# The fifth row block of x^T phi(k) in branch A: seven 64-column products ahead of KV instead of one 128-column pass

## The chip, the cores and the metric

One core of one Trainium2 chip runs the kernel. The metric is the device time of one execution in microseconds; the time before is the median of three runs. The engines are named as in the profile: PE is the matrix engine (PEld its weight loads), DVE the vector engine, ACT the scalar engine, POOL the general one, SP the engine that here only issues transfers. L12 is line 12 of the kernel before.

## The reference

Two linear-attention blocks over the same input x (2048 rows, 640 features, 32 heads of 20) are mixed by a gate:

```python
qkv = (x @ wqkv).reshape(B, S, 3, H, Dh).transpose(2, 0, 3, 1, 4)
q, k, v = qkv
phi = lambda t: where(t > 0, t + 1, exp(t)) + 1e-6
pq, pk = phi(q), phi(k)
kv = einsum("bhsd,bhse->bhde", pk, v)
z = pk.sum(over s)
num = einsum("bhqd,bhde->bhqe", pq, kv)
den = einsum("bhqd,bhd->bhq", pq, z) + 1e-6
block = (num / den).reshape(B, S, D) @ wo
...
g = sigmoid((x * gate_w).sum(-1))
out = g * block_A + (1 - g) * block_B
```

## The kernel before

The sum over the rows, phi(k)^T v, is not taken from v: since v = x wv, the kernel forms G = x^T phi(k), 640 by 640, and then KV = (wv block)^T G for each head group. A head needs only its own 20 columns, so KV is small: six column groups k, each of 60 + 60 or 40 + 40 columns, in 60 products with stationary operands of 60 or 40 columns (`kv_mm`, L457). The two halves of a group lie in the left and the right half of the array's columns (`tile_position=(0, 0)` and `(0, 64)`).

The stages of branch A, in the order of PE's queue:

- k chunks (`k_chunk`, L227): for each of 16 row chunks, 10 products of 320 columns into a PSUM slot, and phi of it. ACT takes the exponential; then either DVE reads the slot again (an unlifted chunk: one `tensor_scalar` and one `scalar_tensor_tensor`), or ACT writes t + 1 (a lifted one, L209) and DVE takes the maximum in SBUF.
- q units (`q_unit`, L275): 10 products of 512 columns each, phi in the same way. The last five units of A stand ahead of G.
- G. The rows of G are the features of x: five blocks of 128. The first four are made by a Strassen-Winograd scheme (`g_strassen`, L375): two by two blocks of x (row half by 256 features) and of phi(k) (row half by 320 columns), seven products of 16 matmuls instead of eight, with sums of x blocks (`x_sum`, S3 and part of MB) and of phi(k) blocks (`k_sum`, in the free buffer pqTB) made on DVE. The fifth block is made the plain way by `g_pass` (L307): 16 row chunks by 2 column halves, 32 matmuls of 320 columns (tile gA). Between its chunks stand `z_pass` (the sums z, tile zA) and DVE's work on them; `rec_pass` (L516) forms the denominators (denA, 40 products four abreast), DVE adds the gate and takes the reciprocal in two halves (`rec(0)`, `rec(1)`), and these go through DRAM into R, which is spread over the partitions.
- `scale` (L576) multiplies phi(q) by R on DVE, in the stage of G and among B's first chunks.
- B's k chunks follow. After the second stands `kv_a` (L480), A's KV with its mask on DVE, and from the fifth on every other chunk is followed by a pair of products for M = KV wo (`m_a`).

Branch B goes through the same stages, and the output is made from both by seven products for each pair of row blocks (`Pair`).

PSUM is one pool of four slots of two banks each (`ps`, L66); a tile in a slot waits until the readers of the one before it are done. k chunks, q units and M products take the slots in turn; the G stage names them. The code in `tc.manual_schedule()` runs in the order in which it is written; each engine goes through its own queue in order. Ahead of everything PE runs seven warm-up products on constants (L164).

Of the kernel before, what the change touches and what calls it, by code (L numbers as in the profile page):

```python
# [8 lines left out]
P = 128  # L9
# [7 lines left out]
DT = D // P  # L17
# [3 lines left out]
HB = 512  # L21
# [11 lines left out]
def kernel(  # L33
# [21 lines left out]
    psum = banks.enter_context(tc.tile_pool(name="psum", bufs=1, space=bass.MemoryType.PSUM))  # L55

    turn = [0]

    def ps_raw(name, slot=None):

        if slot is None:
            slot = turn[0]
            turn[0] = (slot + 1) % 4
        return psum.tile([P, 4 * HB], BF16, tag=f"ps{slot}", name=name)
# [9 lines left out]
    GT2 = persist.tile([P, 2 * DT, HF], BF16, name="GT")  # L74
    GT = [GT2[:, n * DT:(n + 1) * DT, :] for n in range(2)]
# [19 lines left out]
    SX[4] = flat(M[1], "p c d -> p (c d)", ic)  # L95
    TK = [{k: flat(pqT[1], "p c s -> p (c s)", HF, k - 1) for k in (1, 2, 3, 4)}, {}]
# [67 lines left out]
    for n in (HB,) * 6 + (HB // 2,):  # L164
        nc.tensor.matmul(warm[:, 1, 0:n], lhsT=one_l, rhs=one_r[:, 0:n], start=True, stop=True)
# [141 lines left out]
    def g_pass(b, c, slot):  # L307

        pt = ps(f"g{'AB'[b]}", slot)
        for i in range(ST):  # L310
            if b == 0 and i == 4:
                gate_exp()
            if i == (8 if b else 13):
                zsel = z_pass(b)
                if b:
                    p_diff(part[0])
                else:
                    x_sum(2)
                    gate_done(0)
            if b == 1 and i == 13:  # L320
                p_diff(part[1])
# [12 lines left out]
    def x_sum(k, cuts=(0, hc)):  # L334

        x11, x21 = [xn[:, 0:hc, n:n + ic] for n in (0, ic)]
        x12, x22 = [xn[:, hc:ST, n:n + ic] for n in (0, ic)]
        a, b, op = {
            1: (x21, x22, ALU.subtract), 2: (x11, SX[1], ALU.subtract),
            3: (x21, x11, ALU.subtract), 4: (x12, SX[2], ALU.subtract),  # L340
        }[k]
        for lo, hi in zip(cuts, cuts[1:]):
            add_rows(SX[k][:, lo:hi], a[:, lo:hi], b[:, lo:hi], op)
# [21 lines left out]

    def g_prod(pt, left, right, first, lo=0, hi=hc):
# [8 lines left out]
    def g_strassen(b, den):  # L375

        x11, x12 = [xn[:, k:k + hc, 0:ic] for k in (0, hc)]
        x22 = xn[:, hc:ST, ic:2 * ic]
# [4 lines left out]
        def temp(name):  # L383
            return work.tile([P, 2, HF], FP32, tag="osb", name=name, bufs=3)
# [5 lines left out]
        g_prod(even, x11, b11, True, 0, 1 - b)  # L390
        rec = den()
        rec(0)
        g_prod(even, x11, b11, True, 1 - b)
        p1 = temp("p1")
        nc.scalar.copy(out=p1[:], in_=even[:, :, 0:HF])
        if b == 0:
            x_sum(3)
        else:
            rec(1)
        g_prod(odd, SX[2], TK[b][2], True)  # L400
        u2 = temp("u2")
        add(u2[:], odd, p1)
        if b == 0:
            x_sum(4)
        else:
            p_diff(part[2])
            p_diff(part[3])
            m_sum(0)
        g_prod(even, x12, b21, False)
        nc.scalar.copy(out=lo[:, 0:2, :], in_=even[:, :, 0:HF])  # L410
        if b == 0:
            rec(1)
        r_load(b, 1, nc.scalar)
        if b == 0:
            wq[1] = load_w(1, "q", nc.scalar)
        scale(b, 0, 2, 0)
        g_prod(odd, SX[3], TK[b][3], False)
        u3 = temp("u3")
        add(u3[:], odd, p1)
        scale(b, 2, 4, 0)  # L420
        even = ps("gs0", 0)
        g_prod(even, SX[1], TK[b][1], True)
        if b == 1:
            load_wo(1, nc.sync)
        add(hi[:, 2:4, :], even, u3)
        scale(*((b, 0, 2, 1) if b else (b, 4, 5, 0)))
        g_prod(odd, x22, TK[b][4], False)
        if b == 1:
            scale(1, 4, 5, 0)
        add(lo[:, 2:4, :], odd, p1)  # L430
        if b == 1:
            scale(1, 2, 4, 1)
# [3 lines left out]
        if b == 0:  # L436
            scale(0, 0, 2, 1)
    def z_pass(b):
# [454 lines left out]
```

## Time and profile before

| | us |
|---|---|
| runs | 182.18, 182.56, 182.52 (median 182.52) |
| the profiled execution's own time | 182.66 |
| its span | 180.9 |
| k chunks of A from the ninth, and q units, to | 49.2 |
| G of A, 49.2 to | 70.2 |
| B's k chunks with A's KV and M, to | 94.7 |
| B's q units, to | 116.3 |
| G of B, to | 137.3 |
| output, last product to | 177.5 |

All times in the profile are counted from the start of its span. A row of the timeline gives the start, the length, the engine, the line, the operation and its operands; several of one kind in a row are one row with a count. A product's row is longer than the time it holds the array up: products of 320 columns last 299 ns each in the record and follow one another every 136 ns.

### The profile page before, as it was taken

The page shows a single profiled execution, that of the slowest core. Times are in us where ns is not written, and L with a number is a line of the kernel's source. Part 1 is how long each engine was busy: PE and PEld are TensorE (multiplying, and loading weights), DVE is VectorE, ACT ScalarE, POOL GpSimd, SP SyncE. Part 2 cuts the span into 40 slices and gives each one's busy share as a digit, 9 for nine tenths or more (in the row PEclk, how much of TensorE's full clock was granted, in tenths as well). Part 3 has the DMA queues.
Part 4 walks back from the last instruction along what each step waited for, and adds up shares of the span by engine and source line. Part 5 has one row for each costly group of instructions (what it writes and reads, how often), then busy time and mean ns, then how long its engine had stood idle before and what let it go on. Part 6 is the DMA issues. An engine that isn't in the chain of part 4 may idle for free.

```text
span 180.9 us, 3415 instructions
## 1 busy us (share of the span) xinstructions
PE 176.8 (98%) x1340; PEld 119.3 (66%) x1345; DVE 147.6 (82%) x247; ACT 85.8 (47%) x140; POOL 5.4 (3%) x18
## 2 busy tenths in 40 slices
PE   8999999999999999999999999999999999999993
PEld 4565657765577777777775555577777777777772
DVE  0386868989999896888778999969999799977863
ACT  2245846889972101378784779931101763111010
POOL 6000000000000000000000000000002300000000
PEclk9999999999999999999999999999999999999999
DMA  5999999524100217331115000000325451133323
GB/s 183 214 261 170 240 364 297 110 38 145 58 0 5 72 32 226 91 127 35 57 34 186 23 0 0 0 0 18 112 79 144 129 179 60 36 109 112 109 92 127
DMA packets 22842, 19.33 MB, mean 107 GB/s; under 512 B 10538, under 2 KB 22058, under 8 KB 22826
## 3 DMA queue, kind: packets, MB, share of 16 engines
q1 hardware_dynamic: 20744, 16.95, 34.0%
q10 hardware_dynamic: 2082, 2.17, 3.7%
q8 instruction: 10, 0.16, 0.4%
q14 instruction: 6, 0.05, 0.1%
HBM read 12.29 MB, written 4.53 MB: 93 GB/s over the span
## 4 chain that ended last, share of the span: by engine, by line
PE 95%; DMA 2%; issue 0%; DVE 0%; ACTq 0%
PE gs L370 17%; PE kA L218 12%; PE ox L590 12%; PE kB L218 12%; PE qB L281 12%; PE qA L281 6%; PE oz L590 6%; PE qA L291 5%; PE gA L329 2%; PE gB L329 2%; DMA wkA<-in_A_wqkv_dram 2%; PE ow L590 2%; PE qA L301 1%; PE mA L494 1%; PE s L494 1%; PE oy L590 1%
## 5 line engine op out<-in xcount | busy, mean ns | idle before, releaser
L218 PEld LDWEIGHTS <-xT 128*128 128x128 bf16 x320 | 31.0, 98 | 13.1 <-DVE xT L243 0.8
L210 DVE TENSOR_SCALAR e<-e 128x640 bf16<-128x640 bf16 (+2 forms) x53 | 18.9, 357 | 7.2 <-ACT e L205 6.6
L218 PE MATMUL kA<-wkA,xT 128*128 128x320 bf16 (+1 forms) x160 | 22.8, 300 | 0.3 <-DMA wkA<-in_A_wqkv_dram 0.3
L218 PE MATMUL kB<-wkB,xT 128*128 128x320 bf16 x160 | 23.1, 299 | 0.0
L281 PE MATMUL qB<-xT,wqB 128*128 128x512 bf16 x98 | 21.6, 379 | 0.1
L205 ACT ACTIVATE e<-kB 128x640 bf16<-128x640 f32 x16 | 11.3, 704 | 15.8 <-DMA wqB<-in_B_wqkv_dram 9.4
L281 PEld LDWEIGHTS <-wqB 128*128 128x128 bf16 x100 | 11.7, 117 | 9.7
L205 ACT ACTIVATE e<-kA 128x640 bf16<-128x640 f32 x16 | 11.2, 705 | 8.4 <-PE kA L218 8.4
L205 ACT ACTIVATE e<-qA 128x1024 bf16<-128x1024 f32 (+1 forms) x11 | 10.4, 946 | 6.4 <-PE qA L291 5.1
L648 ACT COPY u<-ox 128x320 f32<-128x320 f32 x8 | 3.4, 426 | 20.4 <-PE ox L590 20.4
L205 ACT ACTIVATE e<-qB 128x1024 bf16<-128x1024 f32 x10 | 10.2, 1024 | 5.6 <-PE qB L281 4.9
L370 PEld LDWEIGHTS <-xn 128*128 128x128 bf16 x96 | 9.2, 98 | 3.9 <-issue 0.4
L370 PEld LDWEIGHTS <-S 128*128 128x128 bf16 x96 | 9.4, 98 | 3.6
L281 PE MATMUL qA<-xT,wqA 128*128 128x512 bf16 x49 | 10.9, 379 | 0.1
L214 DVE SCALAR_TENSOR_TENSOR pk<-kB,e 128x640 bf16<-128x640 f32 x12 | 9.9, 825 | 1.3
L590 PEld LDWEIGHTS <-xT 128*128 128x128 bf16 x85 | 8.1, 98 | 2.9
L590 PEld LDWEIGHTS <-pqTB 128*128 128x128 bf16 x80 | 7.8, 98 | 3.2
L590 PEld LDWEIGHTS <-pqTA 128*128 128x128 bf16 x80 | 7.7, 98 | 2.9
L370 PE MATMUL gs<-pk,xn 128*128 128x320 bf16 x64 | 9.5, 299 | 0.0
L281 PEld LDWEIGHTS <-wqA 128*128 128x128 bf16 x50 | 5.9, 117 | 4.8
L291 PE MATMUL qA<-xT,wqA 128*128 128x512 bf16 x38 | 8.9, 379 | 0.1
L212 DVE TENSOR_TENSOR pk<-pk,e 128x640 bf16<-128x640 bf16 x12 | 5.9, 492 | 2.8 <-ACT pk L209 2.2
(123 smaller groups left out, 297.1 us busy)
## 6 DMA issues: line engine op xcount, KB each, us to landing
xn<-in_A_x_dram SPq DMA_DIRECT2D x1, 2240.0 KB, 9.7
out_dram<-pk SPq DMA_DIRECT2D x14, 160.0 KB, 1.8
wvA<-in_A_wqkv_dram SPq DMA_DIRECT2D x1, 800.0 KB
wkB<-in_B_wqkv_dram SPq DMA_DIRECT2D x1, 800.0 KB, 4.6
wqB<-in_B_wqkv_dram ACTq DMA_DIRECT2D x1, 800.0 KB, 5.0
wvB<-in_B_wqkv_dram SPq DMA_DIRECT2D x1, 800.0 KB
MA<-mA_dram SPq DMA_DIRECT2D x1, 800.0 KB, 5.5
MB<-mB_dram SPq DMA_DIRECT2D x1, 800.0 KB
```

Of the source, the lines that this page charges most:

```text
L205: nc.scalar.activation(out=e[:], in_=src, func=ACT.Exp)
L210: nc.vector.tensor_scalar(e[:], e[:], 1.0, EPS, op0=ALU.min, op1=ALU.add)
L212: nc.vector.tensor_tensor(out=dst, in0=dst, in1=e[:], op=ALU.max)
L214: nc.vector.scalar_tensor_tensor(out=dst, in0=src, scalar=1.0 + EPS, in1=e[:], op0=ALU.add, op1=ALU.max)
L218: nc.tensor.matmul(pt[:, hf, 0:w], lhsT=xT[:, c, i * P:(i + 1) * P], rhs=wk[b][:, c, hf * HF:hf * HF + w], start=(c == 0), stop=(c == DT - 1),
L281: nc.tensor.matmul(pt[:, u, :], lhsT=mixed(wq[b][:, c, :], m), rhs=xT[:, c, n * HB:(n + 1) * HB], start=(c == 0), stop=(c == DT - 1),)
L291: nc.tensor.matmul(pt[:, u, :], lhsT=mixed(wq[b][:, c, :], m + u), rhs=xT[:, c, n * HB:(n + 1) * HB], start=(c == 0), stop=(c == DT - 1),)
L329: nc.tensor.matmul(pt[:, hf, 0:HF], lhsT=xn[:, i, c * P:(c + 1) * P], rhs=pk[:, i, hf * HF:(hf + 1) * HF], start=(i == 0), stop=(i == ST - 1),
L370: nc.tensor.matmul(pt[:, n, 0:HF], lhsT=left[:, i, n * P:(n + 1) * P], rhs=right[:, i, :], start=(first and i == 0), stop=(i == hc - 1), s ...
L494: nc.tensor.matmul(dst[:w, 0:HF], lhsT=KVA[:rows, k, 0:w], rhs=wo_sb[b][:rows, k, n * HF:(n + 1) * HF], start=True, stop=True,)
L590: nc.tensor.matmul(dst, lhsT=left[:, c, r0:r0 + P], rhs=right[:, c, :], start=(first and c == 0), stop=(c == DT - 1), skip_group_check=not ...
L648: nc.scalar.copy(out=self.u6[:], in_=self.at("x"))
```

## The change

The diff's core; the rest are shifts of names that follow from it.

```diff
-    psum = banks.enter_context(tc.tile_pool(name="psum", bufs=1, space=bass.MemoryType.PSUM))
+    def psum_pool(stack, name, slots, **how):
+        pool = stack.enter_context(tc.tile_pool(name=name, bufs=1, space=bass.MemoryType.PSUM, **how))
+        pools.update({slot: pool for slot in slots})
+    psum_pool(banks, "low", (2, 3))
+    high = ExitStack()
+    psum_pool(high, "high", (0, 1))
...
-    GT2 = persist.tile([P, 2 * DT, HF], BF16, name="GT")
+    GT2 = persist.tile([P, 2 * (DT + 1), HF], BF16, name="GT")
+    SN = {k: flat(M[0], "p c d -> p (c d)", P // 2, k - 1) for k in (1, 2, 3, 4)}
...
-    for n in (HB,) * 6 + (HB // 2,):
+    for n in (HB // 2,) * 13:
...
+    def narrow_sums():
+        for k in (1, 2, 3, 4):
+            x_sum(k, f0=2 * ic, w=P // 2, dst=SN)
...
+    def g_a(single):
+        odd, even = two("o"), two("e")
+        third = ps("gs2", 2)
+        p1 = g_temp("p1")
+        gate_exp()
+        for n in prod(even, x11, b11, True):
+            nc.scalar.copy(out=p1[:, n], in_=even[n])
+        g_prod(third, SX[1], t[1], True, 0, 5)
+        zsel = z_pass(0, 3)
+        x_sum(2)
+        gate_done(0)
+        g_prod(third, SX[1], t[1], True, 5)
+        rec = rec_pass(0, zsel, 3)
+        rec(0)
+        x_sum(3)
+        for n in prod(even, x12, b21, False):
+            nc.scalar.copy(out=lo[:, n, :], in_=even[n])
+        wq[1] = load_w(1, "q", nc.scalar)
+        u2 = g_temp("u2")
+        for n in prod(odd, SX[2], t[2], True):
+            add(u2[:, n], odd[n], p1[:, n])
+        x_sum(4, 0, hc // 2)
+        u3 = g_temp("u3")
+        for n in prod(odd, SX[3], t[3], False):
+            add(u3[:, n], odd[n], p1[:, n])
+            if n == 0:
+                x_sum(4, hc // 2, hc)
+        for n in range(2):
+            add(hi[:, 2 + n], third[:, n, 0:HF], u3[:, n])
+        for n in prod(odd, x22, t[4], False):
+            add(lo[:, 2 + n], odd[n], p1[:, n])
+        rec(1)
+        g_prod(third, SX[4], b22, False)
+        for n in range(2):
+            add(hi[:, n], third[:, n, 0:HF], u2[:, n])
+        r_load(0, 1, nc.sync)
+        x11, x12, _, x22 = x_blocks(2 * ic, P // 2)
+        def narrow(pt, left, right, first):
+            for i in range(hc // 2):
+                for r in range(2):
+                    rows = slice(r * P // 2, (r + 1) * P // 2)
+                    j = r * hc // 2 + i
+                    nc.tensor.matmul(
+                        pt[rows, :], lhsT=left[:, j, :], rhs=right[:, j, :], start=(first and i == 0),
+                        stop=(i == hc // 2 - 1), tile_position=(0, rows.start), skip_group_check=not first,
+                    )
+        A, B = two("e")
...
+        narrow(A, x11, b11, True)
+        nc.scalar.copy(out=p1, in_=A)
+        narrow(B, SN[2], t[2], True)
+        nc.scalar.copy(out=u6, in_=B)
+        C, G = two("o")
+        narrow(C, x12, b21, True)
+        add(lo[:, DT - 1, :], C, p1)
+        narrow(A, SN[1], t[1], False)
+        nc.scalar.copy(out=p15, in_=A)
+        narrow(B, SN[3], t[3], False)
+        add(hi[:, DT, :], B, p15)
+        narrow(G, SN[4], b22, True)
+        add(v, u6, p15)
+        add(hi[:, DT - 1, :], G, v)
+        kv = ps("kvA", 2)[:, 0]
+        wide = range(DT - 1)
+        kv_step(kv, (0,), wide, True)
+        narrow(B, x22, t[4], False)
+        add(lo[:, DT, :], B, p1)
+        kv_step(kv, (1, 2, 3, 4, 5), wide)
+        kv_step(kv, (0, 1, 2), (DT - 1,))
+        kv_step(kv, (3, 4, 5), (DT - 1, DT))
+        kv_step(kv, (0, 1, 2), (DT,))
+        kv_mask(kv)
...
+    def load_narrow():
+        src = A_wqkv[2 * ic:D, 2 * D:3 * D].rearrange("(n p) f -> p n f", n=2)
+        for r in range(2):
+            nc.sync.dma_start(out=wv[0][r * P // 2:(r + 1) * P // 2, DT - 1:DT + 1, :], in_=src)
...
+        if n:
+            k_sum(0, 1)
...
-                k_sum(0, 1)
+                narrow_sums()
...
-        g_all(0)
-        turn[0] = 3
+        high.close()
+        with late_pool("halves") as halves:
+            g_a(lambda name, n: bank(halves, f"{name}{n}"))
+        psum_pool(banks, "again", (0, 1), reuse_waits="tile")
+        turn[0] = 0
+        scales = {1: (0, 0), 2: (1, 0), 3: (2, 0), 4: (3, 0), 5: (4, 0), 7: (0, 1), 9: (1, 1), 10: (2, 1), 11: (3, 1), 13: (4, 1)}
         for i in range(ST):
-            k_chunk(1, i, lifted=i in (5, 7, 9, 13))
-            if i in (3, 5, 7):
-                scale(0, i // 2 + 1, i // 2 + 2, 1)
+            k_chunk(1, i, lifted=i in (1, 2, 3, 5, 7, 9, 11, 13))
+            if i in scales:
+                c, h = scales[i]
+                scale(0, c, c + 1, h)
             if i > 3 and i % 2 == 0:
                 m_a(i // 2 - 2)
             if i == 1:
-                kv_a()
                 wv[1] = load_w(1, "v", nc.sync)
```

In words. The fifth block (features 512 to 639) is cut into two halves of 64 features and goes through the same seven-product scheme as the other four. A narrow product adds over the eight row chunks of a row half, but four of them go into the left half of the array's columns and four into the right (`r`), so each PSUM tile holds two partial sums on 64 partitions each; eight matmuls of 320 columns make a product, 56 the whole block, against 32 before. The partial sums are added by KV itself: `load_narrow` puts the 64 rows of wv on both halves of the partitions, and the fifth block fills two row tiles of GT, so KV has 72 products instead of 60. The four differences of narrow x blocks lie in the buffer of MA (SN); they are made where the first sum of phi(k) blocks was, which moves ahead of A's second q blocks.

KV no longer stands between B's chunks but directly behind the narrow products, with its first eight matmuls ahead of the seventh of them. The wide products write one-bank tiles (`halves`, laid over slots 0 and 1, in which the first tiles used are those of slot 1; the last q unit is in slot 0), and each half of a product is read by itself. The order around zA is another: the 26 products ahead of zA are now the first wide product and part of a second, and six products instead of eight lie between zA and denA. All rescaling of phi(q) goes behind B's chunks, ten pieces of one row tile and one half each; four more of these chunks are lifted. The second half of R is stored and loaded through SP's queue instead of ACT's, and B's wq is issued earlier on ACT. In the output, the stores of pairs 1 and 2 take both their row blocks in one transfer, and the temporaries u6 and v share one tile. Branch B's G is unchanged.

More of the change, by code (lines that the diff above doesn't have):

```diff
@@ L310, in g_pass @@
         for i in range(ST):
[L311 to L320, printed above, removed]
+            if i == 8:
+                zsel = z_pass(b, 0)
+                p_diff(part[0])
+            if i == 13:
                 p_diff(part[1])
@@ L364, in z_last, with g_half @@
         add_rows(Z[:, 0, 0:HF], Z[:, 0, 0:HF], Z[:, 0, HF:D], ALU.add)
+    def g_half(pt, left, right, n, first, lo=0, hi=hc):
+        for i in range(lo, hi):
+            nc.tensor.matmul(
+                pt, lhsT=left[:, i, n * P:(n + 1) * P], rhs=right[:, i, :],
+                start=(first and i == 0), stop=(i == hc - 1), skip_group_check=not first,
+            )
     def g_prod(pt, left, right, first, lo=0, hi=hc):
@@ new lines, in kv_step @@
+    def kv_step(dst, ks, cs, fresh=False):
+        for k in ks:
+            for c in cs:
+                for p0, hf, d0, w in kv_groups(k):
+                    nc.tensor.matmul(
+                        dst[p0:p0 + w, k * WT[0]:k * WT[0] + w], lhsT=wv[0][:, c, hf * HF + d0:hf * HF + d0 + w],
+                        rhs=GT[hf][:, c, d0:d0 + w], start=(fresh and k == ks[0] and c == cs[0]), stop=(c == cs[-1]),
+                        tile_position=(0, p0), skip_group_check=True,
+                    )
```

140 lines of the change are left out of this document (75 added, 65 removed).

## The prediction

> **What bounds the kernel now.** I read the page from the top: the busy shares, then the chain that ended last, then TensorE's waits, and only then the stage that the change rewrites.
>
> ```profile
> PE 176.8 (98%) x1340; PEld 119.3 (66%) x1345; DVE 147.6 (82%) x247; ACT 85.8 (47%) x140; POOL 5.4 (3%) x18
> ...
> DVE  0386868989999896888778999969999799977863
> ...
> PEclk9999999999999999999999999999999999999999
> ...
> PE 95%; DMA 2%; issue 0%; DVE 0%; ACTq 0%
> ...
> PE xt L165 <- PEq L877: 0.8, 1, 0.8
> PE kA L218 <- DMA wkA<-in_A_wqkv_dram: 0.3, 1, 0.3
> ```
>
> TensorE (PE) is busy for 98% of the span, its clock is granted in full in every slice, and 95% of the chain is its own work. The last two lines are all that its view of waits holds: 1.1 us, both before 6 us. From there to the last product PE never waits. So the time can only fall by work taken from PE, and it can rise by any new wait on PE's queue, however small. VectorE (DVE), at 82%, is the engine that could make one.
>
> The stretch that is rewritten, from the chain in order of time (start, length, what):
>
> ```profile
> 1.24 4.19 DMA wkA<-in_A_wqkv_dram
> ...
> 49.17 3.53 PE gA L329 x26
> 52.70 0.17 PE zA L442 x5
> 52.88 0.82 PE gA L329 x6
> 53.70 0.27 PE gs L370 x2
> 53.98 1.21 PE denA L177 x40
> 55.18 15.05 PE gs L370 x110
> 70.23 2.72 PE kB L218 x20
> 72.94 0.96 PE kvA L462 x60
> 73.91 4.18 PE kB L218 x30
> ```
>
> The fifth row block is gA: 32 full products, 3.53 + 0.82 = 4.35 us, 136 ns each. KV is 60 small products, 0.96 us.
>
> **Part 1: the seven narrow products.** They replace 32 products of 320 columns by 56 whose stationary operand has 64 columns, two of them side by side in the array's column halves. If a pair runs at once, that is 28 pair times for 32. No row shows a 64-column pair of 320; these are the nearest:
>
> ```profile
> 53.91 0.95 PE L177 MATMUL denA<-pqTA,zsel 128*32 128x256 bf16 x28
> ...
> 53.91 1.28 PE L177 MATMUL denA<-pqTA,zsel 128*32 128x256 bf16 x40
> ...
> 72.37 0.57 PE L218 MATMUL kB<-wkB,xT 128*128 128x320 bf16 x3
> ...
> 72.88 0.51 PE L462 MATMUL kvA<-GT,wvA 128*60 128x60 bf16 x22
> ...
> 72.88 1.03 PE L462 MATMUL kvA<-GT,wvA 128*60 128x60 bf16 x60
> ```
>
> The first two rows are the same run of products cut at two places: 12 more take 0.33 us, and they go four abreast, so a round of 256 columns takes 110 ns. One product alone costs 136 ns for 320 columns, 0.43 ns a column; 64 columns more make a round of 320 columns 0.110 + 0.028 = 0.138 us. I take 0.137 us a pair. The other end is the pair one after the other, 0.272 us; denA, which shares the array in the same way, stands against that. 28 x 0.137 = 3.84 us: a saving of 0.51 us, the only one in the change.
>
> **Part 2: KV grows from 60 to 72 products**, because the block now has six row tiles. By the last two rows 38 of them take 0.52 us, 13.7 ns each; 12 more cost 0.17 us (0.19 by 0.96/60). The kB row (0.57 us, three products) puts its third start at 72.64 and kvA's first at 72.88: 0.24 where 0.136 is usual, so entering the split array costs 0.1 us. That is paid once before, at KV, and once after, at the first narrow product, since KV follows in the same form. It is no term.
>
> **Part 3: denA comes two products sooner.** Before, eight products lie between zA and denA (0.82 + 0.27 us); after, six, because the two gs products moved ahead of zA.
>
> ```profile
> 52.27 0.42 DVE L210 TENSOR_SCALAR e<-e 128x1024 bf16<-128x1024 bf16 x1
> ...
> 52.79 0.69 DVE L212 TENSOR_TENSOR pqTA<-pqTA,e 128x1024 bf16<-128x1024 bf16 x1
> ...
> 53.40 0.32 DVE L446 TENSOR_TENSOR zsel<-zA,headE 128x160 bf16<-128x160 f32 x1
> ...
> 53.90 0.99 PEld L177 LDWEIGHTS <-zsel 128*32 128x32 bf16 x40 [0.26 <-DVE zsel L446]
> ```
>
> zsel stands behind the last q unit's work on DVE and cannot come sooner. It ends at 53.72, and its readers began at 53.90. PE would be ready 0.27 us earlier than before, at 53.63. So denA waits between 0.09 us (started at 53.72) and 0.27 (at 53.90); I take 0.18. Behind it in PE's queue stands the whole rest of the stage. The first products themselves wait for nothing: their banks lie where the second q unit was read long ago.
>
> **Part 4: the narrow results must be read while PE runs on.** Five DVE adds and three ACT copies now stand between the products and KV, and two products write banks that must be read first.
>
> ```profile
> 61.80 1.75 DVE L530 RECIPROCAL rT<-d 128x256 bf16<-128x256 f32 x1
> ...
> 70.27 0.89 DVE L435 TENSOR_TENSOR GT<-gs,u 128x320 bf16<-128x320 f32 x2 [1.35 <-PE gs L370]
> ...
> 167.75 0.84 PE L590 MATMUL ox<-TM,xT 128*128 128x320 bf16 x5
> ...
> 167.91 0.48 DVE L595 TENSOR_TENSOR pk<-ox,xn 128x320 bf16<-128x320 f32 x1
> ...
> 168.63 0.43 ACT L648 COPY u<-ox 128x320 f32<-128x320 f32 x1 [2.29 <-PE ox L590]
> ...
> 169.08 0.49 DVE L595 TENSOR_TENSOR v<-u,xn 128x320 f32<-128x320 f32 x1 [0.29 <-ACT u L648]
> ```
>
> A result is read 0.2 us after PE could go on (168.63 less the fifth start, 167.75 + 0.54, less 0.136), an add takes 0.48, a copy 0.43. Count from the first narrow product, 0.55 us each. The second reciprocal goes ahead of this on DVE: it starts at about -1.5, when the wide product before last has been added (-2.18 + 0.2 + 0.48), and with 0.42 us of preparation ends at +0.67; two adds of the wide block end at 1.56. The third product's result is due at 1.84, so 0.28 us are spare. The fifth product ends at 2.74, its add runs 2.94 to 3.42. PE has done the sixth product and eight KV products by 3.40 and starts the seventh at 3.48, with 0.06 for the signal: 0.08 late. DVE then does v, the sixth and the seventh's add, to 4.87; PE reaches the last six KV products at 4.83 and needs 4.93. Together 0.17 us; 0 if DVE overlaps its instructions, as the pair at 70.27 does (0.89 for two), and each 0.1 us that DVE is later beyond the spare costs 0.1.
>
> **Part 5: the rescaling of phi(q) leaves this stage** and goes, in ten pieces, behind B's k chunks. There DVE must keep within four PSUM slots of PE.
>
> ```profile
> 79.76 0.70 ACT L205 ACTIVATE e<-kB 128x640 bf16<-128x640 f32 x1 [0.35 <-PE kB L218]
> ...
> 81.18 0.49 DVE L212 TENSOR_TENSOR pk<-pk,e 128x640 bf16<-128x640 bf16 x1 [0.36 <-ACT pk L209]
> ...
> 81.59 0.69 DVE L579 TENSOR_TENSOR pqTA<-pqTA,R 128x1024 bf16<-128x1024 bf16 x1
> ...
> 82.20 0.32 DVE L210 TENSOR_SCALAR e<-e 128x640 bf16<-128x640 bf16 x1
> ...
> 82.62 0.82 DVE L214 SCALAR_TENSOR_TENSOR pk<-kB,e 128x640 bf16<-128x640 f32 x1
> ...
> 95.89 0.82 DVE L214 SCALAR_TENSOR_TENSOR pk<-kB,e 128x640 bf16<-128x640 f32 x1
> ```
>
> Start to start, a piece takes 0.61, a lifted chunk 0.83 and another 1.22 us, against PE's 1.36 a chunk and 0.27 for each M product. A lifted chunk that is not held up is done 2.03 us after PE (79.76 less 0.2, to 81.59). From chunk 1 on this lag grows: chunk 4 is at 2.66, chunk 5 at 2.47, chunk 6, not lifted and behind two pieces, at 2.94 and 0.08 for signals. Its slot is wanted 2.99 us after it was filled, by the third M product: 0.03 us late; I take 0.05. Later lags stay under 2.9, and the last chunk is lift-bound or level as before (95.89 + 0.82), so B's q pass starts from the same state. ACT has 0.35 us idle in every chunk pair for the four added lifts.
>
> **Part 6: what costs nothing.** The thirteen warm-ups stream the same 3,328 columns as the seven.
>
> ```profile
> 0.84 2.93 PE L165 MATMUL xt<-const-bfloat16-1.0 128*128 128x512 bf16 x7 [0.84 <-PEq L877]
> ...
> 3.42 1.15 PEld L239 LDWEIGHTS <-xn 128*128 128x128 bf16 x10 [0.35 <-DMA xn<-in_A_x_dram]
> ```
>
> Behind them PE waits for x, and the chain there is the load of wkA, to 5.43. Were they 0.3 us longer, that load would still cover them. The Trainium skill ("TensorE: Matmul & The Clock Gate", Part 1) says that the clock opens after some 3.4 us of activity, whatever the number of matmuls; by it too this part is zero. The narrow copy of wv (two more transfers of 160 KB, with wvA cut to 640) follows wo on SP's queue, ahead of B's wk, and is wanted only at the last KV products. R's second store and load go from ACT's queue to SP's, ahead of wvB, which only B's KV reads; R itself is wanted at B's chunk 7, some ten us after its reciprocal. The narrow differences (four of 512 elements) take the place of the first k sum on DVE, which moves into the sixth slice, where DVE is busy six tenths; were there no room, it would pass through four PSUM slots before PE felt it. In the output, u6 and v share a tile with three buffers where each had two, and the stores of pairs 1 and 2 go out together, on a queue for which PE never waits.
>
> **The sum:** -0.51 + 0.17 + 0.18 + 0.17 + 0.05 = +0.06 us. The profiled execution took 182.66 us for a span of 180.9, so 182.72; against the median of the three runs, 182.52, it is 182.6. Less PE work, given back as waits.
>
> **The rivals.**
> *Faster:* the waits of parts 3 to 5 all fall away and a pair costs 0.133: -0.62 + 0.17 = -0.45, 182.1 us. For it speaks that DVE's back-to-back instructions overlap; against it that zsel is bound by DVE. Chance 0.17.
> *Slower, by the weight loads:* each pair needs two 64-column loads; if they can't run ahead in the split array they are added. zA's five products with full weights and 32 columns take 0.17 us, 34 ns each, so unhidden loads cost at most about 34 ns a pair: 28 x 0.171 = 4.79, and the sum is +1.0, 183.5 us. It decides above 0.148 us a pair. denA, whose loads were hidden, is against it. Chance 0.10. The Trainium skill speaks for this one: "TensorE: Matmul & The Clock Gate", Part 3, under what overlaps and what doesn't, lets a weight load run under a product only where the two use other rows of the array, and a column pair uses all of them. The trace does not agree for denA, whose rounds of 110 ns leave no room for four loads.
> *Slower, by DVE's queue at the reciprocal:* if the split adds leave DVE 0.9 us later than part 4 has it, the spare 0.28 is gone and KV ends 0.6 late: 183.2 us. It decides from 0.6 us of delay. Chance 0.15.
> *The pairs don't run together:* 56 x 0.136 = 7.6, +3.8, 186.4 us. Chance 0.03.
> *The backlog in B's chunks* passes on 0.1 us or more at each M product: 183.1 us. Chance 0.05.
>
> **How the numbers follow.** My own case has 0.50: 182.6 us. A measurement of this kernel tells 0.2% (0.37 us) from no change; so faster has 0.17, slower 0.10 + 0.15 + 0.03 + 0.05 = 0.33, the rest is the same. The range, 182.0 to 183.3, takes in the fast case and the DVE one, and leaves out the serial pairs and most of the weight-load case.
>
> **What would show it.** In the changed profile: narrow starts 0.137 us a pair (part 1); denA's weight load released by zsel with PE idle 0.1 to 0.3 us (3); PE idle ahead of the seventh narrow product and the last KV products (4); a wait of an M product for DVE near chunk 8 (5); warm-ups over before x lands (6). Wrong: pairs above 0.148 us, or PE waits of over 0.8 us in all between 49 and 95 us.

## The result, and the profile after

| | runs | median, us | lowest to highest |
|---|---|---|---|
| before | 8 | 182.41 | 182.18 to 182.77 |
| after | 8 | 183.95 | 182.67 to 184.81 |

The ratio is 1.0078, with a 95% interval of 1.005 to 1.0106: the kernel became slower, and its time lies above the range of the prediction. The profiled execution took 183.93 us (before 182.66), and its span is 182.1 us (before 180.9), so 1.2 us have to be found in the trace.

First the page of the changed kernel (busy times and counts, the queue of instruction fetches, and the shares in the chain that ended last):

```profile
PE 177.3 (97%) x1382; PEld 120.7 (66%) x1387; DVE 150.0 (82%) x264; ACT 89.0 (49%) x147; POOL 5.4 (3%) x18
...
q8 instruction: 11, 0.18, 0.5%
...
PE 89%; DVE 5%; DMA 2%; issue 1%; ACT 1%; DVEq 0%
```

Its view of TensorE's waits (total, times, longest):

```profile
PE ow L700 <- DMA MB<-mB_dram: 0.9, 1, 0.9
```

PE does 42 products more, and it has a wait of 0.9 us that the kernel before did not have: the first product with branch B's M (tile MB) waits for MB's load. That is at 151 us in the output, 80 us behind the stage that was rewritten. (The view counts from the end of a product's row, 299 ns behind its start, where the next product usually starts after 136. So it shows 0.16 us less than a wait costs, and short waits not at all.)

Now the span is cut at two places where both kernels do the same, the first of 80 k products in a row and the output's first product. The timeline of the kernel before:

```profile
27.32 11.06 PE L218 MATMUL kA<-wkA,xT 128*128 128x320 bf16 x80
...
137.16 0.84 PE L590 MATMUL ox<-MA,pqTA 128*128 128x320 bf16 x5
```

Of the changed kernel:

```profile
27.25 11.06 PE L226 MATMUL kA<-wkA,xT 128*128 128x320 bf16 x80
...
137.07 0.84 PE L700 MATMUL ox<-MA,pqTA 128*128 128x320 bf16 x5
```

109.84 us before, 109.82 after. All that the prediction summed lies in between, and it comes out 0.02 us ahead. The loss is in the output. The chain of waits there (start, length, what), before:

```profile
137.32 0.68 PE ox L590 x5
...
143.43 2.04 PE ox L590 x15
...
150.90 1.37 PE ow L590 x10
...
165.19 2.04 PE ox L590 x15
...
176.76 0.76 PE ox L590 x5
```

And after:

```profile
137.23 0.68 PE ox L700 x5
...
143.34 2.04 PE ox L700 x15
...
147.41 4.28 DMA MB<-mB_dram
...
151.74 1.52 PE ow L700 x10
...
166.25 2.08 PE ox L700 x15
...
177.95 0.76 PE ox L700 x5
```

From the first row to the last it is 39.44 us and 40.72. From 143.4 to the first `ow` product it is 7.47 and 8.40, and that row itself is 0.15 longer, since PE stood still ahead of it: 1.08 us at MB. The other 0.20 us are spread over the rows of 15 products, many of which take 2.08 instead of 2.04. And -0.02 + 1.08 + 0.20 = 1.26; the 80 k products began 0.07 us sooner than before, which leaves the 1.2 us of the spans.

Why is MB late? SyncE (SP) issues six stores of B's M rows and then the load that reads them back. The timeline of SP's queue, before:

```profile
141.30 3.23 SPq L500 DMA_DIRECT2D mB_dram<-pk  x6
146.36 0.35 SPq L503 DMA_DIRECT2D MB<-mB_dram  x1
```

After:

```profile
141.21 3.99 SPq L610 DMA_DIRECT2D mB_dram<-pk  x6
147.41 0.35 SPq L613 DMA_DIRECT2D MB<-mB_dram  x1
```

The load comes 5.06 us behind the first store before, 6.20 after: 1.14 more. It had nothing to give away. In the kernel before it was issued at 146.36 and landed at 150.71 by the trace's landing events, and the first product that reads it starts 0.04 us later, as the timeline of PE shows:

```profile
150.75 1.52 PE L590 MATMUL ow<-MB,pqTB 128*128 128x320 bf16 x10
```

That is 0.148 us behind the start of the product ahead of it, where 0.136 is usual. (The chain's 150.90 is the end of that product's row.) So whatever delays this load delays PE. The tile's view for the stores gives the shortest, median and longest issue in ns; in the kernel before:

```profile
L500 SPq DMA_DIRECT2D mB_dram<-pk x6: 308/340/382, 141.3 to 144.2; - x6
```

In the changed kernel one issue takes 1,428 ns:

```profile
L610 SPq DMA_DIRECT2D mB_dram<-pk x6: 309/339/1428, 141.2 to 144.9; - x6
```

The DMA view from 141 to 146 us (GB/s in 40 slices of 0.125 us; then the queue of instruction fetches, if it has packets there). Before, without such a packet:

```profile
GB/s 0 0 0 0 0 0 0 0 41 174 174 174 266 359 359 287 338 205 92 164 225 205 215 205 195 256 297 215 82 164 174 225 256 338 318 338 205 10 0 0
```

After:

```profile
GB/s 0 0 0 0 0 0 0 0 123 195 295 256 348 318 266 328 256 41 143 184 236 154 51 10 10 10 10 20 20 21 195 205 205 287 338 338 318 287 389 389
...
q8 instruction: 1, 0.02, 1.9%
```

For a microsecond, 143.75 to 144.75, next to nothing moves. Ahead of that hole an instruction packet of 16,384 bytes begins, at 142.33, and takes 1,549 ns. In the kernel before the packet nearest to the stores begins at 146.19, when they have landed. These packets come once in 256 PE instructions in the mean (232 to 319 matmuls and weight loads between two in these two profiles, but for one of 184), so they are blocks of PE's program; the change puts 42 products with their weight loads, 84 instructions, ahead of this point, and every later block boundary moves forward.

### The profile page after: what moved, and what is told of

Read it like the earlier page. It is cut to its first block, busy times and chain, and to the rows that moved or that the text cites. A ratio compares the mean times of both kernels' runs of the same rounds, so it can differ in the third digit from the quotient of the medians.

```text
span 182.1 us, 3520 instructions
## 1 busy us (share of the span) xinstructions
PE 177.3 (97%) x1382; PEld 120.7 (66%) x1387; DVE 150.0 (82%) x264; ACT 89.0 (49%) x147; POOL 5.4 (3%) x18
## 4 chain that ended last, share of the span: by engine, by line
PE 89%; DVE 5%; DMA 2%; issue 1%; ACT 1%; DVEq 0%
PE kA L226 12%; PE kB L226 12%; PE qB L289 12%; PE ox L700 11%; PE gs L386 10%; PE qA L299 5%; PE oz L700 4%; PE o L377 4%; PE gB L331 2%; DMA MB<-mB_dram 2%; PE qA L289 2%; PE ow L700 2%; DVE GT L656 2%; PE e L465 2%; PE xt L173 2%; DVE pqTA L220 2%
## 5 line engine op out<-in xcount | busy, mean ns | idle before, releaser
L220 DVE TENSOR_TENSOR pk<-pk,e 128x640 bf16<-128x640 bf16 x16 | 7.9, 492 | 2.8 <-ACT pk L217 1.6
L705 DVE TENSOR_TENSOR pk<-ox,xn 128x320 bf16<-128x320 f32 x16 | 7.8, 487 | 0.6 <-PE ox L700 0.6
L386 PEld LDWEIGHTS <-S 128*128 128x128 bf16 x64 | 6.2, 98 | 2.4
L217 ACT ACTIVATE pqTB<-qB,lift 128x1024 bf16<-128x1024 f32 x7 | 7.8, 1108 | 0.0
L222 DVE SCALAR_TENSOR_TENSOR pk<-kA,e 128x640 bf16<-128x640 f32 x8 | 6.6, 825 | 1.1
```

Of the source, the lines that this page charges most:

```text
L217: nc.scalar.activation(out=dst, in_=src, func=ACT.Identity, bias=lift[:])
L220: nc.vector.tensor_tensor(out=dst, in0=dst, in1=e[:], op=ALU.max)
L222: nc.vector.scalar_tensor_tensor(out=dst, in0=src, scalar=1.0 + EPS, in1=e[:], op0=ALU.add, op1=ALU.max)
L386: nc.tensor.matmul(pt[:, n, 0:HF], lhsT=left[:, i, n * P:(n + 1) * P], rhs=right[:, i, :], start=(first and i == 0), stop=(i == hc - 1), s ...
L705: nc.vector.tensor_tensor(out=dst, in0=acc, in1=sb, op=ALU.add)
```

## The experiments

T1: the block fetch falls among the six stores, holds the issue of one, and MB comes late. T2, a rival: the transfers that the change moved on SP's queue are behind it. T3: the tile that u6 and v share costs 0.20 us. A fourth, T4, came up on the way. The indented paragraphs say what was expected of a kernel before it ran.

"Fetch" is the instruction packet nearest to the stores, "hold" the longest issue of the six, "landing to load" the time from the last store's last landing event to MB's load, "first store to load" the two issues, and "pause" the gap between two starts of PE's products at MB's first one (0.136 is none); all from the profiled execution. The ratio is to the kernel before, whose median was 182.47 to 182.66 us in these batches.

| kernel | median, us | ratio [95%] | fetch, us | hold, us | landing to load | first store to load | pause |
|---|---|---|---|---|---|---|---|
| before | 182.41 | | 146.19 | 0.38 | 0.29 | 5.06 | 0.15 |
| after | 183.95 | 1.0078 [1.005, 1.0106] | 142.33 | 1.43 | 0.59 | 6.20 | 1.22 |
| before, 42 k products split | 183.35 | 1.0048 [1.003, 1.0067] | 141.89 | 1.81 | 0.29 | 6.24 | 1.42 |
| before, 42 output products split | 182.72 | 0.9999 [0.9978, 1.0019] | 145.74 | 0.38 | 0.29 | 5.04 | 0.14 |
| after, 40 k products split | 183.13 | 1.0023 [1.0001, 1.0046] | 139.10 | 0.39 | 0.59 | 5.35 | 0.43 |
| after, 96 k products split | 183.19 | 1.0035 [1.0009, 1.0061] | 145.81 | 0.38 | 0.59 | 5.35 | 0.37 |
| before, SP's queue | 182.72 | 1.0014 [0.9992, 1.0035] | 145.87 | 0.39 | 0.39 | 5.13 | 0.22 |
| before, shared tile | 182.86 | 1.0011 [0.9991, 1.003] | 146.05 | 0.38 | 0.29 | 5.02 | 0.14 |
| after, own tiles | 183.52 | 1.005 [1.0033, 1.0068] | 143.22 | 1.81 | 0.59 | 6.52 | 1.62 |
| after, own tiles, 40 split | 182.77 | 1.0001 [0.9981, 1.0021] | 140.09 | 0.38 | 0.59 | 5.38 | 0.39 |
| after, own tiles, 14 split | 182.72 | 1.001 [0.9998, 1.0022] | 139.37 | 0.38 | 0.59 | 5.34 | 0.34 |
| before, wvB in three | 182.78 | 1.0015 [1.0002, 1.0027] | 145.70 | 0.38 | 0.59 | 5.37 | 0.33 |
| after, six transfers more | 183.36 | 1.0064 [1.0037, 1.009] | 142.29 | 1.14 | 0.27 | 5.90 | 0.94 |
| the same, own tiles, 14 split | 183.13 | 1.0029 [1.0017, 1.0042] | 139.87 | 0.48 | 0.27 | 5.39 | 0.44 |
| after, own tiles, 14 split, narrow wv on ACT | 184.40 | 1.0087 [1.0054, 1.0119] | 140.86 | 0.38 | 0.16 | 4.91 | 0.14 |
| after, own tiles, 14 split, R on ACT | 186.42 | 1.0193 [1.0162, 1.0223] | 143.81 | 0.38 | 0.16 | 4.91 | 0.20 |

### The block fetch

Branch B's k products of 320 columns are made in two halves of 160, which follow one another every 69 ns. So 42 split products add 84 PE instructions and only 0.11 us (the stretch from 27 to 137 us).

```diff
         w = HF + (hf if b == 0 else 0)
+        if b == 1 and 0 < c < DT - 1 and halved[0] < 42:
+            halved[0] += 1
+            for lo in (0, HF // 2):
+                nc.tensor.matmul(
+                    pt[:, hf, lo:lo + HF // 2], lhsT=xT[:, c, i * P:(i + 1) * P],
+                    rhs=wk[b][:, c, hf * HF + lo:hf * HF + lo + HF // 2], start=False, stop=False, skip_group_check=True,
+                )
+            return
```

> The kernel before, with 42 products of 320 columns in B's first seven k chunks each made as two of 160 columns: 84 more instructions on PE's queue, as many as the change adds, and nothing else. Theory (PE's own instruction fetch, the 16 KB blocks on queue q8, has moved among the stores of B's M blocks): the block that came at 146.19 us comes between 141 and 144 us, stores of mB land in over 2.5 us instead of 1.9, the load of MB is issued after 147 us and PE waits 0.3 to 2 us for it: 182.9 to 184.2 us. Rival (the changed order of transfers on SP's queue): no wait for MB, 182.4 to 182.6 us, the splits themselves costing 0.1 at most.

The view of waits of this kernel, which is the kernel before in all else:

```profile
PE ow L599 <- DMA MB<-mB_dram: 1.1, 1, 1.1
```

And its timeline of SP's queue:

```profile
140.88 4.42 SPq L509 DMA_DIRECT2D mB_dram<-pk  x6
147.12 0.35 SPq L512 DMA_DIRECT2D MB<-mB_dram  x1
```

The held issue, the late load and the wait are there without any of the change's own parts. The control has the same edit in `prod`, behind MB's first use (from pair 0's `p6` on):

> The kernel before with 42 products split in two as in before_split42, the same 84 added PE instructions, but in the output behind MB's first use. T1: the fetch near 146 us stays where it was, MB's load isn't late, and the time is 182.4 to 182.8 us. Rival, 84 more instructions cost about 0.8 us wherever they stand: 183.3 us.

It costs nothing. Its timeline of SP's queue is that of the kernel before:

```profile
140.99 3.23 SPq L500 DMA_DIRECT2D mB_dram<-pk  x6
146.03 0.35 SPq L503 DMA_DIRECT2D MB<-mB_dram  x1
```

In the changed kernel more instructions should bring the fetch out of the stores again, the opposite of a cost per instruction:

> The changed kernel with 40 products of B's k chunks made in halves, 80 more instructions on PE's queue. Theory (instruction fetch): the block that came at 142.33 us comes before 140.5 us, so the stores of mB land in about 2 us, the load of MB is issued by 146.5 us and PE waits for it under 0.3 us: 182.5 to 182.9 us. Rival (SP's queue): the stores stay slow, 183.6 to 184.2 us.

> The changed kernel with 96 of branch B's k products split in two, 192 more PE instructions ahead of the output, so that the next block boundary, 256 instructions on, comes near 146 us, behind the stores, as in the kernel before. T1: MB's load is issued within 5.3 us of the first store, PE waits for MB not at all or under 0.3 us, time 182.9 to 183.3 us (the cost of the shared tile stays, and 0.1 us for the splits). Rival, each added instruction or product costs: 184.0 us or more.

With 80 more the fetch is ahead of the stores, with 192 more the next one comes behind their issue, and both times the hold is gone and some 0.8 us with it. T1 is shown, but the first run is a little above what T1 had for it, and in both the load is still 0.3 us later than before the change.

The hold ends with the fetch. In the four kernels with a held issue (after; before with 42 k products split; after with own tiles; after with six transfers more) this issue ends 0.39, 0.37, 0.38 and 0.38 us behind the end of the fetch packet, about the length of a usual issue (0.34), whether it began 0.5 us into the fetch or 0.1 us ahead of it. Data already on their way are late too: in the changed kernel the last landings of the first two stores, both issued ahead of the fetch, come 3.93 and 3.88 us behind their issue, against 1.97 and 2.02 before.

### SP's queue alone

```diff
-            eng = nc.scalar if h else nc.sync
+            eng = nc.scalar if h and b else nc.sync
...
-        r_load(b, 1, nc.scalar)
+        r_load(b, 1, nc.scalar if b else nc.sync)
...
-    wv[0] = load_w(0, "v", nc.sync)
+    wv[0] = load_w(0, "v", nc.sync, (0, 1, 3, DT))
```

> The kernel before with SP's queue as in the changed one: A's second store and load of R go through SP's queue instead of ACT's, and wvA comes in three transfers instead of one. PE's queue is unchanged. Theory (instruction fetch): no wait for MB, 182.3 to 182.6 us. Rival (SP's queue): stores of mB land late, the load of MB is issued after 147 us, 183 us or more.

No issue is held and no landing late, so T2 is not the cause of the large loss. MB's load comes 0.1 us later and PE pauses 0.08 us longer than before, and the median is 0.1 us above what was expected; that is due to the number of transfers, as the last series shows.

### The shared tile

```diff
 (the kernel before, shared)
-            self.u6 = tmp("u6", "ex")
-            nc.scalar.copy(out=self.u6[:], in_=self.at("x"))
+            u = work.tile([P, 2, HF], FP32, tag="osb", name="u", bufs=3)
+            self.u6, self.v = u[:, 0], u[:, 1]
+            nc.scalar.copy(out=self.u6, in_=self.at("x"))
 (the changed kernel, own tiles)
-            u = g_temp("u")
-            self.u6, self.v = u[:, 0], u[:, 1]
-            nc.scalar.copy(out=self.u6, in_=self.at("x"))
+            self.u6 = tmp("u6", "ex")
+            nc.scalar.copy(out=self.u6[:], in_=self.at("x"))
...
+            self.v = tmp("v", "zr")
```

> The kernel before with u6 and v in one shared tile with three buffers, and nothing else of the change. T3: the 15-product rows of the output's chain go from 2.04 to 2.08 us and the time from 182.55 to 182.7 to 182.9 us; the block fetch stays at 146 us and PE doesn't wait for MB. Rival, the shared tile costs nothing and the whole loss is the fetch: 182.5 to 182.6 us, rows of 2.04.

> The changed kernel, with u6 and v of the output in tiles of their own (one buffer for u6, two for v) instead of the two halves of one tile. Theory (the shared tile makes ACT's copy of u6 wait through an instruction ahead of it, 0.03 to 0.05 us on each of seven products that need its bank): these gaps close, 0.2 to 0.3 us less than the changed kernel. The instruction fetch does not move, so the wait for MB stays. Rival (the gaps are only DVE's lag after the late load of MB): the gaps stay.

The medians can't settle 0.2 us; the chains can. The kernel before with the shared tile:

```profile
165.33 2.08 PE ox L590 x15
```

The changed kernel with own tiles:

```profile
166.83 2.04 PE ox L700 x15
```

One edit brings the 2.08, the other takes it away. Behind 153 us the kernel before loses 0.11 us in three pauses (0.15 to 0.20 from start to start where 0.136 is usual); with the shared tile, in either kernel, it is 0.33 to 0.34 in nine. T3 is shown as an effect; why the shared tile makes ScalarE's copy later was not tried. As a time the kernel with own tiles says little: its fetch did not stay where it was but came at 143.22 us, and its pause at MB was 1.62 us instead of 1.22.

### Fetch and tile out

> The changed kernel with both suspected costs out: u6 and v in tiles of their own, as before the change, and 40 of branch B's k products made as two of 160 columns, which adds 80 PE instructions ahead of the output. T1 (PE's own instruction block is fetched while the six mB stores are under way, so that MB's load starts late) and T3 (u6 and v in one tile cost 0.04 us at each of some seven products): the block is fetched near 139 us, MB's load is issued within 5.3 us of the first store, PE doesn't wait for MB, the runs of 15 products between evacuations take 2.04 us and not 2.08; time 182.3 to 182.8 us. Rival, the changed G stage itself costs the time later on: 183.1 or more, as with either of the two parts alone.

> The changed kernel with u6 and v in tiles of their own and only 14 of branch B's k products split, 28 PE instructions more, which should bring the fetch about 1.3 us forward, to 141.0 to 141.8 us, just as the six stores begin. T1 by a hole (while the block is fetched, next to no data of the stores moves, and the stores that are issued later catch up): the first stores land late, the last ones nearly on time; PE waits for MB 0 to 0.6 us; time 182.4 to 183.1 us. Rival, any fetch that touches the stores costs all of it: wait 0.9 us or more, 183.4 us or more as with no products split.

Both are near the kernel before (1.0001 and 1.001), but PE still pauses at MB. In the second the fetch came ahead of the stores and not at their beginning, so it doesn't tell what a fetch does that meets them in part.

### SP's 79th instruction

In the changed kernel and all its variants so far it takes 0.59 us from the last landing to the load, in the kernel before 0.29. The chain of waits of SP's instructions in the changed kernel with own tiles shows where:

```profile
145.49 1.90 DMA mB_dram<-pk
147.39 0.02 issue
147.40 0.03 SPq L613
147.43 0.46 issue
147.89 0.03 SPq L613
147.92 0.06 issue
147.98 4.37 DMA MB<-mB_dram
```

The store has landed, the wait is passed, and then SP does nothing for 0.46 us before its last wait, for a semaphore that had long been there. T4 as first put: the order of the waits, which differs between the two kernels, since the last store gets another DMA semaphore.

```diff
 (the kernel before: two transfers more, the changed kernel's order)
-                wv[1] = load_w(1, "v", nc.sync)
+                wv[1] = load_w(1, "v", nc.sync, (0, 1, 3, DT))
 (the changed kernel: six more, the order of before)
-    wk[1] = load_w(1, "k", nc.sync)
+    wk[1] = load_w(1, "k", nc.sync, (0, 1, 3, DT))
...
-                wv[1] = load_w(1, "v", nc.sync)
+                wv[1] = load_w(1, "v", nc.sync, (0, 1, 2, 3, 4, DT))
```

> The kernel before with branch B's wv loaded in three transfers and not one: two transfers more ahead of the mB stores, so that the last store takes the DMA semaphore that it takes in the changed kernel, and SP's waits ahead of MB's load stand in the changed kernel's order (the last store third of four, not first). T4: SP then needs 0.55 to 0.6 us from the last store's landing to the load, not 0.30; the load is issued 5.3 to 5.4 us behind the first store (5.06 in the kernel before), PE's pause ahead of MB's first product is 0.25 to 0.45 us; time 182.6 to 182.9 us. Rival, the order of the waits costs nothing: 5.0 to 5.15 us, no pause, 182.4 to 182.6.

> The changed kernel with nothing but the six more transfers: the order of SP's waits as before the change, the fetch among the stores and the shared tile as after it. T4 with T1: the load 5.8 to 6.2 us behind the first store if the fetch hits the stores (6.20 after, less 0.3, with a hold of 1.1 to 1.5 us), time 183.4 to 183.8 us. Rival, the order of the waits is all of the late load: 5.0 to 5.1 us, no pause at MB, 182.7 us.

> The changed kernel with all three suspected costs out: own tiles for u6 and v, 14 of branch B's k products split (fetch ahead of the stores, 139 to 141 us), and B's wv and wk loaded in five and three transfers, six more, which puts the last store's semaphore first among SP's waits as in the kernel before. T4: the load 5.0 to 5.1 us behind the first store (5.34 without the six transfers), no pause of PE at MB, output as long as before (first to last product's start 40.8 us), time 182.3 to 182.6 us. Rival, the 0.3 us have another cause: 5.3 us or more and a pause of 0.3 us stay.

The first two came as T4 had them (the second's time 0.04 us below its range). The third did not: from landing to load it took 0.27 us, but the fourth store was issued 0.43 us late, by the same pause of 0.46 us in another place. In every profile of the table the pause stands behind SP's 79th recorded instruction: just behind MB's load in the kernel before (where it harms nobody), just ahead of SP's last wait in the changed kernel, which has two SP instructions more by then, and ahead of the fourth store with the six transfers, which make eight more still. So the pause goes by the place and not by the order. The next run has the changed order and the old place, with the narrow transfers of wv issued from ScalarE's queue:

```diff
-            nc.sync.dma_start(out=wv[0][r * P // 2:(r + 1) * P // 2, DT - 1:DT + 1, :], in_=src)
+            nc.scalar.dma_start(out=wv[0][r * P // 2:(r + 1) * P // 2, DT - 1:DT + 1, :], in_=src)
```

> The changed kernel with own tiles for u6 and v, 14 of branch B's k products split, and the two narrow transfers of wv issued from ScalarE's queue instead of SyncE's. SP has two instructions fewer ahead of MB's load, so that its 79th recorded one is the load itself, as in the kernel before; the order of SP's waits is still that of the changed kernel (the last store third of four). T4 by position (SP pauses 0.46 us behind its 79th instruction, whatever stands there, as in all profiles so far): 0.29 us from the last landing to the load, the load 5.0 to 5.1 us behind the first store, no pause of PE at MB if the fetch stays ahead of the stores, output 40.8 to 40.9 us long, time 182.3 to 182.6 us. Rival, T4 by the order of the waits: 0.59 us, 5.35 us, a pause of 0.3 us, 182.7 us.

Its timeline of SP's queue:

```profile
142.43 3.23 SPq L619 DMA_DIRECT2D mB_dram<-pk  x6
147.34 0.35 SPq L622 DMA_DIRECT2D MB<-mB_dram  x1
```

4.91 us, no pause of PE, and the output as short as before (40.79 us between its first and last product's start, 40.80 before, 42.08 after). T4 by place is shown. (Landing to load is 0.16 us and not the expected 0.29: when the last store lands, two of SP's four waits are left, in the kernel before all four.) The time itself was missed by far, 184.40: the two transfers went out on ScalarE's queue at 4 us, and the 80 k products began at 28.44, 1.2 us later. The last try put A's R there instead:

> The changed kernel with own tiles for u6 and v, 14 of branch B's k products split, and all four transfers of A's R (two stores, two loads) issued from ScalarE's queue, none from SyncE's: MB's load is again SP's 79th recorded instruction, and the narrow transfers of wv are back on SyncE's queue, where they don't delay the start. The output as in the kernel before (40.8 us from its first product's start to its last's, no pause of PE at MB), 109.8 us from the 80 k products to the output if the issues on ScalarE's queue delay nothing in G, time 182.3 to 182.7 us. If the gain of the changed G stage is worth what the stretch shows (0.02 us), it can't be told from the kernel before. Rival: the pause at MB stays (0.3 us, output 41.0), or ScalarE's issues in G cost 0.3 us or more.

The output was nearly right again (40.85 us, the pause 0.07 us longer than none), but the rival for G came true: ScalarE's queue stood behind the load of R, as its view of PE's waits shows:

```profile
PE e L474 <- ACT pn L484: 2.3, 1, 2.3
```

That is not all of the loss. Behind this wait PE's granted clock falls, in the page's slices from 69 to 79 us:

```profile
PEclk9999999999999997899999999999999999999999
```

From 71.5 us on it is one half for 3.4 us. The stretch from the 80 k products to the output takes 113.67 us, 3.85 more than in the changed kernel: 2.3 are the wait, and most of the rest is the clock. Five of the six runs have the same mean clock, 0.991; the sixth, at the full clock, took 184.75 us.

So with all three causes out the output is that of the kernel before, and no kernel tried here beats it.

### Three stores on ScalarE's queue

The odd ones of the six mB stores were issued from ScalarE's queue, in the kernel before and in the changed one with own tiles:

```diff
+        eng = nc.scalar if b and k % 2 else nc.sync
-        nc.sync.dma_start(out=m_dram[b][rows, :], in_=part[:w].rearrange("p b n -> p (b n)"))
+        eng.dma_start(out=m_dram[b][rows, :], in_=part[:w].rearrange("p b n -> p (b n)"))
```

> The kernel before with three of the six mB stores (odd k) issued from the ScalarE queue and not from SyncE's. A control for the next run: the fetch stays at 146 us; MB's load is issued within 0.5 us of where it was; 182.3 to 182.9 us, more only if issuing delays ScalarE's copies.

> The changed kernel with u6 and v in tiles of their own, and three of the six mB stores issued from the ScalarE queue. If the fetch holds up only the queue that is issuing just then, by making SyncE's issue of one store 1.4 us long, the other queue's stores go on, MB's load is issued within 5.5 us of the first store, and the time is 182.5 to 182.9 us. If it holds up the transfers of all queues, the load is as late as with one queue (6.2 us or more behind the first store), PE waits about 1 us, and the time is 183.3 us or more.

184.09 us (1.0087 [1.0072, 1.0103]) and 183.48 (1.0054 [1.0037, 1.007]). The control is slower by itself: ahead of MB's first product PE loses 0.96 us in four gaps that the kernel before does not have, and another 0.55 at MB. The view of waits lists the longest of the four, which ends with a copy of ScalarE's; the other three are too short for it. The second kernel has the same four gaps (0.93 us) and none at MB, so its time says nothing of the fetch. That came at 141.22, with the first stores only. Which queues a fetch holds up stays open.

## Why the prediction was wrong

The forecast was 182.6 us with a range to 183.3. The median is 183.95. The step that failed is part 6, "what costs nothing": it put three costs at nothing that come to 1.28 us.

- It priced the added instructions by their time and not by their number. 84 more PE instructions put a block fetch among the mB stores, and two more SP instructions put SP's 79th ahead of MB's load. Neither the stores nor the load are touched by the change, and the prediction did not look at them. Of the 1.14 us by which the load is later, 0.30 are SP's pause (0.59 less 0.29) and 0.84 the hold. It makes 1.08 us of PE's time. The late load without the change: 1.0048 with the PE instructions alone, 1.0015 with the SP instructions alone.
- "From there to the last product PE never waits" was read from a view that can't show a short wait. MB's load landed 0.04 us ahead of the first product that reads it, so a delay of this load had to show.
- It named the moved SP transfers and asked only whether what they carry is wanted later, which it isn't. The "queue for which PE never waits" is SP's, and it carries MB's load.
- "u6 and v share a tile with three buffers where each had two" was priced at nothing and costs 0.20 us.

The chance of 0.33 for slower went to other mechanisms (weight loads, the reciprocal, B's chunks), and none of them came. Nor did the signs named as refuting it: no pair over 0.148 us, no long waits between 49 and 95 us. They watched the rewritten stretch only. The sum's own parts held:

**Part 1** (0.137 us a pair). The timeline of the narrow products in the changed kernel, eight matmuls or four pairs to a product:

```profile
66.45 0.71 PE L465 MATMUL e<-pqTB,MA 128*64 128x320 bf16 x8
...
68.62 0.71 PE L465 MATMUL o<-pk,MA 128*64 128x320 bf16 x8
69.17 0.28 PE L504 MATMUL kvA<-GT,wvA 128*60 128x60 bf16 x8
69.45 0.73 PE L465 MATMUL e<-pqTB,xn 128*64 128x320 bf16 x8
69.99 1.12 PE L504 MATMUL kvA<-GT,wvA 128*60 128x60 bf16 x64
71.04 0.72 PE L226 MATMUL kB<-wkB,xT 128*128 128x320 bf16 x4
```

From 66.45 to 69.17 are 20 pairs in 2.72 us, 0.136 each, though each pair loads two sets of weights. So the rival of exposed weight loads fell, and with it, for this case, the rule of the Trainium skill ("TensorE: Matmul & The Clock Gate", Part 3) that spoke for it, by which a weight load overlaps a running product only where the row groups differ.

**Parts 2 and 4** (0.17 each). The first eight KV products take 0.28 us to the next start and need 0.11 at part 2's 13.7 ns, so the seventh narrow product waits at most 0.17. The other 64 take 1.05 us with the way back to full weights, which leaves no room for a second wait of size.

**Part 3** (0.18). The changed kernel's timeline of weight loads:

```profile
53.70 0.56 PEld L185 LDWEIGHTS <-zsel 128*32 128x32 bf16 x24 [0.40 <-DVE zsel L562]
```

0.40 us idle where it was 0.26: 0.14 more, released by zsel as foreseen.

**Part 5** (0.05). In the chain B's k chunks take from 71.11 to 94.60, 23.49 us; before it was 70.23 to 94.69 less KV's 0.96, 23.50. The backlog cost nothing.

Together, by the stretch from 27 to 137 us, -0.02 us where the sum had +0.06.

## What to carry to other kernels

An edit's instructions count by their time and by their number: each one shifts all later places in its engine's stream, and with them a block fetch or a pause that can meet a transfer far behind the edit. So go along the whole chain for transfers that land just before they are wanted (here a load that landed 0.04 us ahead of its first reader), and ask of every edit how those could come late. To tell a stage's own worth from such an accident, shift the instructions by splits that cost nothing and measure again, and compare the stretches of the two traces rather than the times.

## What the runs showed of the hardware

- A block fetch of PE's instructions took 0.88 to 2.03 us in these traces. The Trainium skill ("Runtime: NRT & Kernel Launch", Instruction fetch mechanics) has blocks of 256 instructions too, and calls the cost of crossing a boundary "mostly hidden". For PE the traces agree; for another engine's stores they don't: one issue was held for 1.14 to 1.81 us instead of 0.34 in four kernels, each time until the fetch was over.
- Not every issue within a fetch is held. MB's load went out at 146.36 in the kernel before, inside a fetch from 146.19 to 147.07, in the usual 0.35 us, and so it did in five more kernels of the table; in the changed kernel the first store inside the fetch took 0.31 us and the next was held. Why stays open.
- The fetch doesn't keep step with PE exactly: three kernels with the same products ahead of it had it at 141.22, 142.33 and 143.22 us, while the 80 k products began within 0.3 us. That this makes the changed kernel's runs spread over 2.1 us (before 0.6) is likely, but not shown: a fetch is seen only in the one execution of a kernel that was profiled.
- SP stood still for 0.46 us behind its 79th recorded instruction, whatever that was: a wait, a load or a store's wait. What it does then, the profile does not show.
